# Moving attention bursts of the first tile pair to earlier places between its matmul groups

## The chip, the cores and the metric

The kernel runs on one core of one Trainium2 chip. The metric is the device time of one execution in microseconds (us). Changed and unchanged kernel are compared by the medians of their runs.

## The reference

Chunked attention feeds a feed-forward layer. Eight batches, 8 heads, 576 positions, head size 64; every chunk of 64 positions attends only to itself.

```python
scores = scale * np.matmul(q_c, k_c.transpose(0, 1, 2, 4, 3))
scores = scores - np.max(scores, axis=-1, keepdims=True)
attn = np.exp(scores)
attn = attn / (np.sum(attn, axis=-1, keepdims=True) + 1e-09)
out = np.matmul(attn, v_c)
...
h = x @ w_in
g = np.where(pos, h, np.where(neg, 0.0, (h + beta) ** 2 / (4.0 * beta)))
return (g @ w_out).astype(np.float32)
```

`x` is the attention output as 4608 tokens by 512; `w_in` is 512 x 2048, `w_out` 2048 x 512; `pos` is h >= 1 and `neg` is h <= -1.

## The kernel before, in words

The tokens are cut into nine tiles of 512 (`t` = 0 to 8). Attention is done in 36 units: one unit is one tile and one pair of heads. Unit n has two parts on TensorE (PE in the profile): its scores (L480, 32 small matmuls) and, after a softmax on VectorE (DVE) and ScalarE (ACT), its values (L502, 32 small matmuls). Operands of the feed-forward layer are split into a high and a low part, so that each product of 128x128 by 128x512 takes three matmuls.

Tiles 0 to 2 are computed plainly (L625, L661). Tiles 3 to 8 are computed as three pairs, (3, 4), (5, 6), (7, 8), by a scheme with seven products of half size in place of eight. A pair has two stages:

- **h**, 56 groups (L918): for each of eight blocks p of `w_in`, seven groups of six matmuls. DVE and ACT turn the results into activations (L939, L945, L948, L949).
- **outputs**, 56 groups (L1124): for each of the seven products in `OUT_ORDER = ("P1", "P2", "P6", "P5", "P7", "P3", "P4")`, eight groups of six matmuls. ACT and DVE make the operands (L743, L747). After P7, the pieces of the next pair's operands are split between the groups as well.

So a pair has 112 groups, and the kernel calls the position just before group n its place n: places 0 to 55 lie in h, 56 to 63 in P1, 64 to 71 in P2, 72 to 79 in P6, 80 to 87 in P5, and so on. The weights of each group come from DRAM into a ring of ten buffers (`RING`). The Pool queue issues one load of 256 KB per group (L896 in h, L891 in the outputs) as soon as the group ten before it has ended.

The attention of later tiles is put between these groups in bursts. `turns` lists sixteen of them, from unit 20 on, and `between(t, n)` takes the next from the list when n is one of the places in `BURSTS`, first entry for the first pair, second for the second. A burst for units (n, n+2) consists of:

- PE: the values of unit n and the scores of unit n+2, 64 small matmuls in one go.
- DVE and ACT: the softmax of unit n+2: maximum (L536), its scaling (L541), eight exponentials with sums (ACT, L547), sum and reciprocal (L565, L566), multiplication (L571), transposition (L588). ACT copies the values of unit n out of PSUM (L743). DVE transposes q and k of unit n+3 (L456).
- DMA on SP's queue: v of unit n+2 (two, L398), q and k of unit n+4 (four each, L382), and four of the eight moves of the softmax result into the place where the values product reads it (`aT`, L580). The other four moves are on Pool's queue, among the ring loads.

The values of unit n+2 need the `aT` moves of both queues, two bursts later. q, k, v, aT, maxima and sums have two buffers each, the transposed q and k one, and the two PSUM banks `ps_a` are shared by scores and values.

Each engine works its instructions in a fixed order. It is found before the launch by a list scheduler (`Plan.emit`), which gives each step a cost and takes, on each engine, the step that stands first in program order among those that are ready in its own account of time. A step written for a later place can so be taken earlier on its engine, if everything ahead of it is not ready in that account.

Of the kernel before, what the change touches and what calls it, by code (L numbers as in the profile page):

```python
# [134 lines left out]
def kernel(  # L135
# [826 lines left out]
        return f"h_{f}", lambda: held["h"][:, f, :]  # L962

    LATER = -60
    BURSTS = ((10, 17, 24, 38, 45, 52, 59, 68), range(3, 53, 7))
    sums = {
        (name, p): dram.tile([P, 2, QC], F32R, name=f"sums_{name}_{p}")
        for name in OUT_ORDER for p in range(NQ)
# [320 lines left out]
    def burst(n, m):  # L1289
        some = [values_of(*AT[n])] if n is not None else []  # L1290
        if m is not None:
            some.append(scores_of(*AT[m]))
        attn_products(*some, lag=0.8)
        if m is not None:
            attn_softmax(*AT[m])
        if n is not None:
            attn_split(*AT[n])
        if m is not None and m > 3 * NP and m + 1 < ALL:
            attn_turn(*AT[m + 1])
        if n is not None and n + 2 < ALL:  # L1300
            load_heads(*AT[n + 2], "v")
        if m is not None and m + 2 < ALL:
            load_heads(*AT[m + 2], "qk")
# [46 lines left out]
    def between(t, n):  # L1350
        if turns and n in BURSTS[(t - ALONE - 1) // 2]:
            burst(*turns.pop(0))
# [80 lines left out]
```

## Time and profile before

| | us |
|---|---|
| median of 3 runs | 806.91 |
| lowest, highest | 805.44, 808.49 |
| the profiled execution's own time | 805.89 |
| its span, first to last instruction | 804.1 |

The span is that of the profiled execution, 1.8 us less than its own time. Starts in the rows are us from the start of the span. A PE row of a timeline merges matmuls that follow each other; its length reaches to the modelled end of the last one, so the pace is read from one start to the next.

### The profile page before, as it was taken

Reading aid. Unit: us, or ns where it says so; the run is one execution under the profiler, and the core shown is the slowest. Engines: PE = TensorE matmul, PEld = TensorE weight load, DVE = VectorE, ACT = ScalarE, POOL = GpSimd, SP = SyncE. Lnnn points to the kernel's source line nnn. Section 1 sums busy time; section 2 is a strip of 40 time slices with the busy share of each in tenths; the row PEclk is TensorE's granted clock in tenths of the full one; section 3 lists DMA queues with packets and bytes.
Section 4 is the critical chain, followed back from the end, with each engine's and each line's share of the span. In section 5 each row is a group of like instructions: output and inputs, shape, how many; then the busy total and the mean of one; then the engine's idle time right before and its main releaser. Section 6 shows DMA issues by size and latency. Waiting matters only on the chain.

```text
span 804.1 us, 16928 instructions
## 1 busy us (share of the span) xinstructions
PE 795.0 (99%) x5652; PEld 652.8 (81%) x5652; DVE 650.2 (81%) x1131; ACT 537.7 (67%) x1293; POOL 345.5 (43%) x606
## 2 busy tenths in 40 slices
PE   8999999999999999999999999999999999999997
PEld 8887788888888888888888788888888888888886
DVE  5999996768799996686899996777996955589962
ACT  5799975455576775687894665887845556686450
POOL 2122223565655464554455334545343334433340
PEclk9999999999999999999999999999999999999999
DMA  9899843887998897999999899977686896666775
GB/s 223 249 302 239 221 78 127 252 261 228 293 255 225 199 283 207 302 264 250 259 246 273 217 245 256 257 230 214 184 214 197 223 243 195 194 191 195 218 200 118
DMA packets 289495, 181.51 MB, mean 226 GB/s; under 512 B 242945, under 2 KB 254721, under 8 KB 289409
## 3 DMA queue, kind: packets, MB, share of 16 engines
q0 software_dynamic: 40640, 122.72, 48.0%
q1 hardware_dynamic: 244544, 56.93, 33.7%
q10 hardware_dynamic: 4224, 0.79, 0.6%
q8 instruction: 45, 0.74, 0.4%
q14 instruction: 42, 0.34, 0.1%
HBM read 133.17 MB, written 38.80 MB: 214 GB/s over the span
## 4 chain that ended last, share of the span: by engine, by line
PE 84%; DMA 5%; DVE 4%; SPq 3%; ACT 2%; issue 2%; POOL 1%; DVEq 0%; POOLq 0%; ACTq 0%
PE ps_o L1124 17%; PE ps_o L661 15%; PE ps_h L625 15%; PE ps_h L918 13%; PE ps_o L918 13%; PE ps_h L1124 7%; PE ps_a L502 2%; SPq L382 2%; DVE new_wi L747 2%; PE ps_a L480 2%; DMA v_sb<-in_v_dram 1%; DMA k_sb<-in_k_dram 1%; DMA words<-in_moe_w_in_dram 1%; DMA q_sb<-in_q_dram 1%; DMA ring_r<-sums_P 1%
## 5 line engine op out<-in xcount | busy, mean ns | idle before, releaser
L747 DVE TENSOR_TENSOR new_wi<-new_wi,new_wi 128x512 fp32r<-128x512 f32 (+2 forms) x191 | 121.4, 668 | 13.7 <-ACT new_wi L743 12.0
L743 ACT CAST new_wi<-new_wi 128x512 fp32r<-128x512 f32 x157 | 94.3, 626 | 56.8 <-DVE new_wi L747 28.9
L625 PE MATMUL ps_h<-xh,parts 128*128 128x512 f32 x384 | 129.8, 398 | 0.0
L661 PE MATMUL ps_o<-parts,gh 128*128 128x512 f32 x384 | 118.2, 389 | 0.0
L580 POOL DMA_DIRECT2D aT<-e x96 | 50.6, 534 | 80.4 <-DVE r L636 46.0
L625 PEld LDWEIGHTS ps_h<-xh,parts 128*128 128x128 f32 x384 | 72.0, 188 | 16.0
L661 PEld LDWEIGHTS ps_o<-parts,gh 128*128 128x128 f32 x384 | 72.1, 188 | 15.0
L661 PE MATMUL ps_o<-parts,gl 128*128 128x512 f32 x192 | 74.7, 389 | 0.0
L949 DVE SCALAR_TENSOR_TENSOR new_wi<-h,new_wi 128x512 f32<-128x512 f32 x63 | 42.3, 683 | 26.1 <-ACT new_wi L948 26.1
L547 ACT ACTIVATE e<-ps_a,mx 128x64 f32<-128x64 f32 x168 | 50.8, 327 | 11.3 <-DVE mx L541 8.2
L948 ACT ACTIVATE new_wi<-new_wi 128x512 f32<-128x512 f32 x84 | 51.2, 627 | 1.2
L625 PE MATMUL ps_h<-x_parts,parts 128*128 128x512 f32 x128 | 50.1, 391 | 0.9 <-DVE x_parts L610 0.9
L945 ACT ACTIVATE new_wi<-h 128x512 f32<-128x512 f32 x63 | 39.4, 632 | 17.0 <-DVE h L939 17.0
L644 ACT CAST gh<-r 128x512 fp32r<-128x512 f32 x48 | 29.8, 620 | 30.0 <-DVE r L636 18.9
L661 PEld LDWEIGHTS ps_o<-parts,gl 128*128 128x128 f32 x192 | 36.0, 188 | 7.5
L747 DVE TENSOR_TENSOR new_wi<-new_wi 128x512 f32<-128x512 f32 (+2 forms) x64 | 39.4, 629 | 0.5
L636 DVE SCALAR_TENSOR_TENSOR r<-ps_h,r 128x512 f32<-128x512 f32 x48 | 32.6, 680 | 8.8 <-ACT r L635 8.6
L646 DVE TENSOR_TENSOR gl<-r,gh 128x512 fp32r<-128x512 f32 x48 | 32.7, 683 | 8.0 <-ACT gh L644 5.8
L1124 PE MATMUL ps_o<-new_wi,new_wo 128*128 128x512 f32 x156 | 37.6, 390 | 0.0
L580 POOL DMA_DIRECT2D aT<-x x48 | 24.7, 519 | 29.6 <-issue 13.8
L632 ACT ACTIVATE r<-ps_h 128x512 f32<-128x512 f32 x48 | 29.0, 604 | 11.8 <-PE ps_h L625 11.8
L547 ACT ACTIVATION_READ_ACCUMULATOR e<-ps_a,mx 128x1 f32 x168 | 36.7, 218 | 0.0
(232 smaller groups left out, 2074.9 us busy)
## 6 DMA issues: line engine op xcount, KB each, us to landing
ring_r<-combos POOLq DMA_DIRECT2D x36, 256.0 KB, 3.6
new_wo<-sums_P POOLq DMA_DIRECT2D x36, 256.0 KB, 3.2
new_wi<-combos POOLq DMA_DIRECT2D x34, 256.0 KB, 4.2
new_wi<-sums_P POOLq DMA_DIRECT2D x34, 256.0 KB, 3.5
ring_gh<-combos POOLq DMA_DIRECT2D x33, 256.0 KB, 3.7
ring_gl<-combos POOLq DMA_DIRECT2D x33, 256.0 KB, 3.8
ring_gh<-sums_P POOLq DMA_DIRECT2D x33, 256.0 KB, 3.9
ring_gl<-sums_P POOLq DMA_DIRECT2D x33, 256.0 KB, 3.4
```

The source lines that it names most:

```text
L547: nc.scalar.activation(out=e3[:, n, :], in_=sc[:, n // 4, n % 4, :], func=AF.Exp, bias=mx[:, n, :], scale=SCALE, accum_out=sm[:, n, :],)
L580: queues[queue].dma_start(out=aT[b:b + Q, to], in_=x[a:a + Q, of])
L625: nc.tensor.matmul(out=ps, lhsT=weight["wi", j][:, half, kc * P:(kc + 1) * P], rhs=x, start=(kc == 0 and i == 0), stop=(kc == KC - 1 and i ...
L646: plan.add("dve", 0.6, lambda: nc.vector.tensor_tensor(out=gl, in0=now(r), in1=gh.bitcast(F32), op=ALU.subtract), (rkey, ghkey), (glkey,), ...
L661: nc.tensor.matmul(out=acc, lhsT=x[:, cols], rhs=weight["wo", j][:, half, :], start=(j == 0 and i == 0), stop=(j == NF - 1 and i == 2),)
L743: "act", cost, lambda: nc.scalar.copy(out=out(), in_=src()), reads, writes, ahead=ahead
L747: plan.add("dve", cost, lambda: nc.vector.tensor_tensor(out=out(), in0=one(), in1=two(), op=op), reads, writes, port=True, ahead=ahead)
L918: nc.tensor.matmul(out=ps, lhsT=w()[:, at:at + P], rhs=y(), start=name in FRESH and i == 0 and k == 0, stop=i == 1 and k == 2, skip_group_ ...
L945: plan.add("act", 0.52, lambda: nc.scalar.activation(out=now(r), in_=h(), func=AF.Relu, bias=0.5, scale=0.5), (hkey,), (rkey,), ahead=50)
L948: plan.add("act", 0.52, lambda: nc.scalar.square(out=now(r), in_=now(r)), (), (rkey,), ahead=50)
L949: plan.add("dve", 0.6, lambda: nc.vector.scalar_tensor_tensor(out=now(r), in0=h(), scalar=1.0, in1=now(r), op0=ALU.max, op1=ALU.min), (hke ...
L1124: nc.tensor.matmul(out=acc, lhsT=w[:, half, b], rhs=x(), start=name in alone and p == 0 and k == 0, stop=p == NQ - 1 and k == 2, skip_grou ...
```

## The change

One tuple: the places of the eight bursts in the first pair, tiles 3 and 4.

```diff
     LATER = -60
-    BURSTS = ((10, 17, 24, 38, 45, 52, 59, 68), range(3, 53, 7))
+    BURSTS = ((10, 17, 24, 31, 38, 45, 52, 59), range(3, 53, 7))
```

The bursts are handed out in order, so the fourth, for units (23, 25), goes from place 38 to 31, the fifth from 45 to 38, the sixth from 52 to 45, the seventh, (26, 28), from 59 (in P1) to 52 (in h), and the eighth, (27, 29), from 68 (in P2) to 59 (in P1). The second pair's places stay.

## Rows read from the trace of the kernel before

**Rows 1.** The page: busy time and share by engine, and PE's granted clock.

```profile
PE 795.0 (99%) x5652; PEld 652.8 (81%) x5652; DVE 650.2 (81%) x1131; ACT 537.7 (67%) x1293; POOL 345.5 (43%) x606
PEclk9999999999999999999999999999999999999999
```

**Rows 2.** PE's waits over the whole span: us in total, times, longest (last of six, the only one after 100 us).

```profile
PE ps_o L1124 <- DVE new_wi L747: 0.2, 1, 0.2
```

**Rows 3.** PE's timeline, first pair: start, us, what, [idle before].

```profile
315.68 0.84 PE L918 MATMUL ps_h<-lows,new_wo 128*128 128x512 f32 x3
...
317.04 0.61 PE L661 MATMUL ps_o<-parts,gh 128*128 128x512 f32 x2
...
322.48 0.84 PE L918 MATMUL ps_h<-lows,new_wo 128*128 128x512 f32 x3
...
345.65 0.69 PE L502 MATMUL ps_a<-aT,v_sb 64*64 64x64 f32 x32
...
356.49 0.69 PE L502 MATMUL ps_a<-aT,v_sb 64*64 64x64 f32 x32
...
374.03 1.64 PE L918 MATMUL ps_h<-new_wi,ring_gh 128*128 128x512 f32 x6
375.51 1.52 PE L918 MATMUL ps_h<-new_wi,ring_r 128*128 128x512 f32 x6
376.96 0.69 PE L502 MATMUL ps_a<-aT,v_sb 64*64 64x64 f32 x32
...
437.97 0.69 PE L502 MATMUL ps_a<-aT,v_sb 64*64 64x64 f32 x32
...
441.92 2.98 PE L1124 MATMUL ps_o<-new_wi,new_wo 128*128 128x512 f32 x12
444.74 0.61 PE L1124 MATMUL ps_o<-new_wi,new_wi 128*128 128x512 f32 x2
445.52 2.56 PE L1124 MATMUL ps_o<-new_wi,new_wi 128*128 128x512 f32 x10 [0.17 <-DVE new_wi L747]
447.92 2.88 PE L1124 MATMUL ps_o<-new_wi,ring_r 128*128 128x512 f32 x12
450.63 1.52 PE L1124 MATMUL ps_o<-new_wi,ring_gh 128*128 128x512 f32 x6
...
486.00 0.84 PE L918 MATMUL ps_h<-low,new_wi 128*128 128x512 f32 x3
```

**Rows 4.** Busy us by stretch: PE, PEld, DVE, ACT, POOL, clock, DMA share, GB/s.

```profile
356.40:367.30 10.90, 10.90 (x108) 9.08 (x108) 8.63 (x16) 9.23 (x29) 5.82 (x12) 1.00 1.06 260
367.30:376.90 9.60, 9.60 (x43) 7.56 (x41) 5.34 (x8) 6.29 (x12) 5.34 (x11) 1.00 1.08 274
376.90:387.80 10.90, 10.90 (x107) 8.83 (x107) 8.63 (x16) 9.27 (x29) 4.20 (x8) 1.00 0.85 219
...
423.00:437.90 14.90, 14.90 (x125) 12.21 (x124) 14.82 (x28) 7.49 (x25) 8.38 (x16) 1.00 1.10 264
```

**Rows 5.** SP queue's timeline from the second burst of the pair on.

```profile
348.58 1.25 SPq L398 DMA_DIRECT2D v_sb<-in_v_dram  x2
...
356.98 3.61 SPq L580 DMA_DIRECT2D aT<-x  x4
360.69 1.08 SPq L398 DMA_DIRECT2D v_sb<-in_v_dram  x2
...
368.59 3.01 SPq L580 DMA_DIRECT2D aT<-e  x4
377.68 0.95 SPq L398 DMA_DIRECT2D v_sb<-in_v_dram  x2
```

**Rows 6.** DMA issues between 367 and 378 us: count, KB, median us to landing.

```profile
ring_gh<-combos POOLq DMA_DIRECT2D x2, 256.0 KB, 5.3
...
aT<-e SPq DMA_DIRECT2D x4, 32.0 KB, 5.2
```

**Rows 7.** DVE's timeline in the third burst of the pair, its idle time.

```profile
362.94 0.17 DVE L565 TENSOR_SCALAR sm<-sm 128x8 f32<-128x8 f32 x1 [1.83 <-ACT e L547]
```

## The prediction

> **What bounds the kernel now.** I read the page first. PE is busy for 795.0 of 804.1 us and its granted clock stays at full, the 2.4 GHz level, in all forty slices [rows 1]; so the question is only whether PE has idle time that a move can give back or cause. PE's list of waits has six entries, and only one is later than 100 us: 0.2 us on DVE in an output group [rows 2]. The reader is to see that nothing in the pairs waits on the attention.
>
> A busy PE can still hide idle time shorter than a matmul, because its ends are modelled. So I went to PE's timeline and counted starts [rows 3]. The 24 matmuls of tile 2 from 317.04 to 322.48 take 5.44 us, 0.2267 each, so a group of six takes 1.36 us. Two bursts seven groups apart start at 345.65 and 356.49, 10.84 us; less 7 x 1.36 = 9.52 a burst costs PE 1.32 us. The first pair reaches from 315.68 to 486.00, 170.32 us. In it lie 112 groups (152.32), those 24 matmuls (5.44), and nine bursts (11.88): eight of its own and, at 437.97, the one for units (28, 30), which is written for place 3 of the second pair and was taken far sooner. Sum 169.64. All idle time of PE in the stage is therefore 0.68 us, and I find most of it [rows 3]: two matmuls from 444.74 to 445.52 take 0.78 instead of 0.45 (0.33, the wait on DVE), the twelve from 441.92 take 2.82 instead of 2.72 (0.10), the six from 374.03 take 1.48 instead of 1.36 (0.12).
>
> **What the change moves.** Bursts are alike and are handed out in order. For PE, the eight places before and after differ in one: 31 in place of 68. The order of units does not change. So the change adds one burst before group 31, takes one away before group 68, and between the two everything on PE is 1.32 us later; after group 68 it is where it was. PE's work: +1.32 - 1.32 = 0.
>
> *DVE and ACT.* The same seven groups cost DVE 8.63 us with a burst and 5.34 without, ACT 9.23 and 6.29 [rows 4]: a burst is 3.3 us of DVE and 2.9 of ACT. The stretch from place 31 to 38, now 9.6 us with 5.34 of DVE, becomes 10.9 with 8.6, like its neighbours, which have no PE wait and where DVE even stands idle 1.83 us for the exponentials [rows 7]. The cover is this slack of 2.3 us; were it gone, the 3.3 us of DVE would push back activations, which the output operands need only after place 56. In the outputs, DVE is full around the removed burst, 14.82 of 14.9 us [rows 4], and it is DVE that PE waits for at 445.52. With 3.3 us less to do before, DVE is there earlier, and the 0.33 and 0.10 go: -0.4 us. Bounds: 0 (scheduler refills the hole) and -0.68 (all idle time of the stage). I take -0.4.
>
> *SP's queue.* Each burst puts 14 DMAs on it, and it works them in order. The `aT` moves, which the values product two bursts later waits for, stand behind v, q and k there. This is the one resource that has less room after the change. Place 31 falls at 356.49 + 10.84 = 367.33. Its `aT` moves are issued from 356.98 to 360.59 [rows 5]; a move lands 5.2 us after its issue [rows 6], the last of the four is issued about 0.9 before the end, so it lands near 364.9, 2.4 us early. Place 38 falls at 378.17; its moves end at 371.60, landing near 371.60 - 0.75 + 5.2 = 376.05, 2.1 us early (before, they were needed one burst after 376.96, at 387.8 [rows 3]). From here on SP no longer has the pause between 371.60 and 377.68 [rows 5], and each round of 14 must fit in 10.84 us. A round took 12.11 us from 348.58 to 360.69 and 10.91 from 360.69 to 371.60 [rows 5]. With the short round the moves for places 45, 52 and 59 land near 387.0, 397.9 and 408.8, for products at 389.01, 399.85 and 410.69: always 1.9 us or more early. With the long one they land at 388.2, 400.3 and 412.4: 0.9 early, 0.4 late, 1.7 late. A late move stops the burst on PE and with it every group behind it, and nothing gives that back. Bounds: 0 and +1.7 us. I take 0: the long round fell where the DMA engines were full (a share of 1.06 and more), and already in the round from 376.9 the share was 0.85 [rows 4], though that one had its loads close behind each other too.
>
> *Pool's queue and the ring.* The burst's four `aT` moves on Pool stand among the ring loads. A ring load is issued when the group ten before has ended, and lands 5.3 us later in the full stretch [rows 6]; it has nine groups, 12.2 us, so 6.9 us are left. The moved burst can eat some of that, not all: 0.
>
> The Trainium skill, DMA: Bandwidth & Descriptors, section Issuing engines are not separate DMA queues, says that DMAs started by SP, ACT and Pool all run on the same 16 engines and interleave; by it, loads of a burst brought into h slow the ring loads there. By that rule alone PE would lose time only where a ring load needs over 12.2 us, and the sum would stay.
>
> **Sum.** 0 (PE) - 0.4 (DVE's stall) + 0 (SP) + 0 (ring) = -0.4 us. The profiled execution took 805.89 us, its span 804.1; it becomes 805.5. The median of the three runs is 1.0 above that execution, so I forecast 806.9 - 0.4 = 806.5. About 0.5%, 4.0 us, is what a measurement of this kernel can tell from no change, so this is "same".
>
> **Rivals.**
>
> *The hole is refilled.* The scheduler already took burst (28, 30) far ahead of its place. With place 68 empty it may take that burst, or (29, 31) too, into the outputs earlier, so that DVE there is as full as before and the stall stays. For it: the row at 437.97. Against it: nothing firm. 806.9 us. Chance 0.13.
>
> *SP falls behind (the other side).* The place is the burst at 52 or 59, which waits for the `aT` moves. With rounds of 12.1 us it costs up to 1.7 us: 808.6, still within 0.5%. It makes the kernel slower by 4.0 us from the point where 376.05 + 3 x round passes 410.69 + 4.0, a round of 12.9 us, over 0.9 us for each DMA issue; by 5 us it is 811.9. For it: two rounds in a row without a pause, one of them over 10.84. Against it: the four bursts at places 38 to 59 of before stood as close and ran without a PE wait on `aT` [rows 2]. Chance 0.08 for a loss below 4 us, 0.06 for more.
>
> *More idle time than the rows show.* The Trainium skill, Perfetto Trace Analysis, section Tensor Engine Instruction (MATMUL, LD_WEIGHTS), says that the end of a matmul in a profile is an estimate; by it the 99% proves nothing, and a gain of several us could hide in it. The pace of the starts leaves 0.68 us in the stage, whatever the ends are, and it is 1.36 per group where DVE is full as in the rest. A gain of 4 us would have to come from another stage: 802.5 us. Chance 0.02.
>
> **How the numbers follow.** The forecast has 0.71, the rivals 0.13, 0.14 and 0.02. Faster by over 0.5%: 0.02. Slower by over 0.5%: 0.06. The rest is same: 0.92. For the range, the runs of before reach from 1.5 below their median to 1.6 above it; a median lies further inside, so I take 1.6 for the spread on both sides. Below, the bound of -0.68 adds 0.3: 806.5 - 0.3 - 1.6 = 804.6. Above, the bounds of DVE's stall (0.4) and of SP (1.7) add 2.1: 806.5 + 2.1 + 1.6 = 810.2.
>
> **What would show it.** Right: L502 rows on PE near 367.3 and 378.2, none near 423; the same 170 us between the first L918 group of the first and of the second pair; DVE in the stretch after 367 at about 8.6 of 10.9 us; no wait of 0.3 us near 445. SP's pause before 377.68 is gone. Wrong: a PE wait ahead of L502 on `aT` (SP too slow), or on a ring buffer; the stall at 445 still there, with a burst close before it (refilled); a PE wait on DVE at the end of h, where bursts 45 to 59 meet the first output operands.

## The result, and the profile after

The changed kernel is slower: its median is 810.9 us over 13 runs (810.01 to 817.26) against 806.91 over 13 runs of the kernel before, 4.0 us less. By the medians that is a ratio of 1.0049; the ratio on record, worked out over all runs, is 1.0066 with a 95% interval of 1.0052 to 1.0079. The forecast was 806.5 with a range up to 810.2, and "slower by over 0.5%" had a chance of 0.06. The profiled execution, at 810.18 us one of the shorter ones, has a span of 808.4 us, 4.3 more than before. Six of the thirteen runs took 812.64 us or more; what they lost beyond this is not shown by any profile.

The page answers to [rows 1]: PE does the same work at the same clock, so the 4.3 us are time in which it had none.

```profile
PE 794.7 (98%) x5652; PEld 653.1 (81%) x5652; DVE 651.0 (81%) x1131; ACT 538.5 (67%) x1293; POOL 345.8 (43%) x606
...
PEclk9999999999999999999999999999999999999999
```

PE's list of waits (us in total, times, longest) answers to [rows 2]. The late wait on DVE is gone. In its place stand three waits ahead of L502, the values product.

```profile
PE ps_a L502 <- DMA q_sb<-in_q_dram: 2.8, 1, 2.8
...
PE ps_a L502 <- DMA aT<-x: 1.0, 1, 1.0
PE ps_a L502 <- DMA aT<-e: 0.7, 1, 0.7
```

PE's timeline shows where they fall; it answers to [rows 3].

```profile
315.25 0.84 PE L918 MATMUL ps_h<-lows,new_wo 128*128 128x512 f32 x3
...
366.90 0.69 PE L502 MATMUL ps_a<-aT,v_sb 64*64 64x64 f32 x32
...
367.99 0.73 PE L918 MATMUL ps_h<-new_wi,new_wo 128*128 128x512 f32 x2
...
376.29 1.52 PE L918 MATMUL ps_h<-new_wi,ring_r 128*128 128x512 f32 x6
378.48 0.86 PE L502 MATMUL ps_a<-aT,v_sb 64*64 64x64 f32 x29 [0.67 <-DMA aT<-e]
...
399.00 1.52 PE L918 MATMUL ps_o<-new_wi,new_wo 128*128 128x512 f32 x6
401.53 0.86 PE L502 MATMUL ps_a<-aT,v_sb 64*64 64x64 f32 x29 [1.01 <-DMA aT<-x]
...
411.17 1.52 PE L1124 MATMUL ps_o<-new_wi,ring_gh 128*128 128x512 f32 x6
415.47 0.86 PE L502 MATMUL ps_a<-aT,v_sb 64*64 64x64 f32 x29 [2.78 <-DMA q_sb<-in_q_dram]
...
416.78 0.50 PE L1124 MATMUL ps_o<-new_wi,ring_gl 128*128 128x512 f32 x1
...
448.22 2.88 PE L1124 MATMUL ps_o<-new_wi,new_wi 128*128 128x512 f32 x12
450.94 2.88 PE L1124 MATMUL ps_o<-new_wi,ring_r 128*128 128x512 f32 x12
...
489.02 0.84 PE L918 MATMUL ps_h<-low,new_wi 128*128 128x512 f32 x3
...
493.19 0.69 PE L502 MATMUL ps_a<-aT,v_sb 64*64 64x64 f32 x32
```

The moved burst, at 366.90, starts on time. Six matmuls start in 1.36 us, and the last one ahead of a burst takes 0.09 more, so the burst after 376.29 was due at 377.74 and began at 378.48: 0.74 late. In the same way the one after 399.00 lost 1.08 and the one after 411.17 lost 2.85: 4.67 us. The undisturbed burst takes 1.09 us from its first small matmul to the next group (366.90 to 367.99), the one at 415.47 takes 1.31: a burst that waited also runs some 0.2 longer. Why it does is not shown.

The balance of the stage, by the terms of the prediction: it now reaches from 315.25 to 489.02, 173.77 us, with 112 groups (152.32), the 24 matmuls of tile 2 (5.44) and eight bursts (10.56), since the burst for (28, 30) now runs at its own place, at 493.19. That leaves 5.45 us idle, against 0.68 before: 4.77 more. The stage began 0.43 earlier, and what follows it takes 319.38 us in place of 318.10, 1.28 more, which is nearly the 1.32 of the burst that left the stage. So 4.77 - 1.32 + 1.28 - 0.43 = 4.30, the whole difference of the spans.

SP's timeline answers to [rows 5]. One round is v, q, k and then the moves of `aT`.

```profile
335.10 1.12 SPq L398 DMA_DIRECT2D v_sb<-in_v_dram  x2
338.63 2.34 SPq L382 DMA_DIRECT2D q_sb<-in_q_dram  x4
...
349.19 1.08 SPq L398 DMA_DIRECT2D v_sb<-in_v_dram  x2
...
362.57 1.12 SPq L398 DMA_DIRECT2D v_sb<-in_v_dram  x2
...
372.43 2.56 SPq L580 DMA_DIRECT2D aT<-e  x4
375.09 1.08 SPq L398 DMA_DIRECT2D v_sb<-in_v_dram  x2
...
386.30 1.10 SPq L398 DMA_DIRECT2D v_sb<-in_v_dram  x2
...
397.09 0.94 SPq L398 DMA_DIRECT2D v_sb<-in_v_dram  x2
398.40 3.96 SPq L382 DMA_DIRECT2D q_sb<-in_q_dram  x4
402.45 5.02 SPq L382 DMA_DIRECT2D k_sb<-in_k_dram  x4
407.57 1.02 SPq L398 DMA_DIRECT2D v_sb<-in_v_dram  x2
408.69 3.23 SPq L580 DMA_DIRECT2D aT<-e  x4
```

From v to v the rounds take 14.09, 13.38, 12.52, 11.21 and 10.79 us; bursts are due every 10.84. The first round holds a pause of 2.4 us ahead of its q, at 338.63; from there to the end of these rows the queue never pauses for more than 0.9 us. The four moves issued from 372.43 landed by 378.38, a tenth of a microsecond before the burst at 378.48. In the last stretch the moves for the burst at 415.47 stand behind two loads of v and eight of q and k, and are issued from 408.69 to 411.92; the last landed at 415.23. The list of waits names q_sb there, but it is this landing that the start follows. Nor is it the softmax that is late: for the three bursts that waited, DVE had written the transposed exponentials at 365.56, 388.20 and 402.66, and SP issued their moves from 372.43, 394.17 and 408.69, 6.0 to 6.9 us later.

The stretch after the moved burst, and DMA issues between 367 and 378 us, answer to [rows 4, 6] (columns as there):

```profile
366.90:377.70 10.80, 10.80 (x107) 8.83 (x106) 8.64 (x16) 9.13 (x29) 5.74 (x12) 1.00 1.13 260
```

```profile
ring_gh<-combos POOLq DMA_DIRECT2D x2, 256.0 KB, 6.2
```

From 366.90 on DVE has 8.64 us of work in 10.80, as forecast. The DMA engines are full, with a share of 1.13 against 1.08 in the stretch after place 31 of before. These ring loads land 6.2 us after their issue, 5.3 in the same window before [rows 6], and PE does not wait on the ring.

### The profile page after: what moved, and what is told of

Same layout as the page of the kernel before. It is cut to its first block, busy times and chain, and to the rows that moved or that the text cites. A ratio compares the mean times of both kernels' runs of the same rounds, so it can differ in the third digit from the quotient of the medians.

```text
span 808.4 us, 16938 instructions
## 1 busy us (share of the span) xinstructions
PE 794.7 (98%) x5652; PEld 653.1 (81%) x5652; DVE 651.0 (81%) x1131; ACT 538.5 (67%) x1293; POOL 345.8 (43%) x606
## 4 chain that ended last, share of the span: by engine, by line
PE 85%; DMA 5%; ACT 5%; SPq 2%; DVE 1%; issue 1%; POOL 0%; ACTq 0%; DVEq 0%; POOLq 0%
PE ps_o L1124 20%; PE ps_o L661 14%; PE ps_h L625 14%; PE ps_o L918 12%; PE ps_h L918 12%; PE ps_h L1124 8%; PE ps_a L502 2%; DMA q_sb<-in_q_dram 2%; PE ps_a L480 2%; DMA aT<-x 1%; ACT e L547 1%; SPq L382 1%; DMA k_sb<-in_k_dram 1%; ACT words L334 1%; DMA words<-in_moe_w_in_dram 1%
## 5 line engine op out<-in xcount | busy, mean ns | idle before, releaser
L632 ACT ACTIVATE r<-ps_h 128x512 f32<-128x512 f32 x48 | 29.0, 605 | 12.9 <-PE ps_h L625 12.9
L580 POOL DMA_DIRECT2D aT<-x x48 | 24.7, 520 | 26.9 <-issue 13.2
```

Source lines behind the costliest of these rows:

```text
L580: queues[queue].dma_start(out=aT[b:b + Q, to], in_=x[a:a + Q, of])
```

## The experiments

Each is an edit of the changed kernel, compared with the kernel before on the same chip, whose median there was 807.04 us for four of them and 806.49 for the other four. The theory is that SP's in-order queue hands out the `aT` moves too late.

**Is it the density of the bursts?** The first kernel sets them eight groups apart, the last at 66.

```diff
-    BURSTS = ((10, 17, 24, 31, 38, 45, 52, 59), range(3, 53, 7))
+    BURSTS = ((10, 18, 26, 34, 42, 50, 58, 66), range(3, 53, 7))
```

> The changed kernel with the eight bursts evenly eight groups apart, at 10, 18, 26, 34, 42, 50, 58 and 66: the same number of bursts, 12.2 us apart in place of 10.84. Theory A: a round of 14 DMAs of 10.5 to 12.5 us fits, waits of 0 to 0.5 us in all, 806.3 to 807.3. Theory B: six bursts still stand in h and one early in the outputs, DVE and ACT are as full there, 808.5 or more. Theory C: the DMA engines get 12% more time per burst, so it predicts as A does.

Measured 806.68 us (12 runs), ratio 0.9995 (0.9982 to 1.0009), and no wait of PE on the attention in the pairs above 0.15 us. Eight groups apart would be 8 x 1.36 + 1.32 = 12.20 us, but by their starts on PE the bursts stand 12.20, 10.84, 10.84, 15.11, 11.03, 13.76 and 12.20 apart, since the scheduler took some of them a group or two sooner. So there is a gap again, behind the fourth:

```profile
369.09 0.69 PE L502 MATMUL ps_a<-aT,v_sb 64*64 64x64 f32 x32
...
384.20 0.69 PE L502 MATMUL ps_a<-aT,v_sb 64*64 64x64 f32 x32
```

SP's rounds take 12.91, 11.96, 10.98 and 10.19 us from v at 349.92. The earlier places are harmless when the queue gets 1.4 us more a round on average (12.28) and one gap; this run does not part the two.

The second experiment puts only the last burst back to 68.

```diff
+    BURSTS = ((10, 17, 24, 31, 38, 45, 52, 68), range(3, 53, 7))
```

> The changed kernel with the eighth burst back at its place of before, 68, and the fourth to seventh one place sooner. Theory A: the seven close rounds stay, so the waits of the fifth and seventh burst stay (0.74 and 1.08), and the last, 2.85 us, goes since SP has nine groups more: 808.0 to 808.8 us. Theory B: the wait belongs to the end of h, which is as crowded; 810 or more.

Measured 808.71 (12 runs), ratio 1.0023 (1.0007 to 1.0039). Its profile is of one of its longer runs (810.62). By the starts in it the first pair loses 0.16 at 379, 0.74 at 390 and 1.25 at 402, and the large last wait is gone. The arrears were there before place 59 and only grew to it.

The third keeps the burst at 31 and leaves the double gap behind it, between 31 and 45.

```diff
+    BURSTS = ((10, 17, 24, 31, 45, 52, 59, 66), range(3, 53, 7))
```

> The changed kernel with the pause put back, but one burst later than in the kernel before: places 10, 17, 24, 31, 45, 52, 59 and 66. If SP's queue only needs one double gap to work off its arrears (four close bursts, then four): at most 0.3 us of waits, 806.3 to 807.2. If it is the burst at place 31 by itself that is bad: 809 or more.

Measured 806.34 (10 runs), ratio 1.0003 (0.9992 to 1.0013). PE waits on no attention in the pairs; the stall on DVE near 445 is back with 0.22 us, and so is the early burst for (28, 30), at 438.47. SP's timeline of this kernel:

```profile
349.60 1.47 SPq L398 DMA_DIRECT2D v_sb<-in_v_dram  x2
...
362.82 1.09 SPq L398 DMA_DIRECT2D v_sb<-in_v_dram  x2
...
374.50 1.10 SPq L398 DMA_DIRECT2D v_sb<-in_v_dram  x2
...
383.23 2.42 SPq L580 DMA_DIRECT2D aT<-e  x4
388.99 0.94 SPq L398 DMA_DIRECT2D v_sb<-in_v_dram  x2
```

Two rounds in a row are too long again (13.22 and 11.68), but after the moves at 383.23 to 385.65 the queue stands still until 388.99: the gap has paid the arrears. Place 31 is not the harm; that no gap comes after it is. The second pair of the changed kernel fits this: its bursts also stand seven groups apart and its rounds are too long (12.22, 12.11 and 11.54 us from v at 496.65), but after these three there are no more q and k to load, and PE does not wait.

**Is it SP's queue?** All eight `aT` moves of the later tiles go to Pool's queue.

```diff
-                queue = "pool" if t == 1 or j else "sp"
+                queue = "pool" if t == 1 or t > ALONE or j else "sp"
```

> The changed kernel, with the four aT moves of each later burst issued on Pool's queue in place of SP's, beside the four that are there already; same bytes, same places. Theory A (SP's queue: the moves stand behind v, q and k, and a round of 14 DMAs takes longer than the 10.84 us between bursts): the moves leave soon after the softmax, PE's three waits ahead of L502 (0.74, 1.08, 2.85 us) go, 806.3 to 807 us. Theory B (the softmax itself is late, since DVE and ACT are full at the end of h): the waits stay, 810 to 811. Theory C (all 16 DMA engines are full, so that the moves land late from whichever queue): at least 2 us of waits stay, 808.5 or more, or ring loads come late in their place.

Measured 814.19 (6 runs), ratio 1.008 (1.0057 to 1.0102): the gain that the theory of SP expected did not come, and ring loads came late, as the third theory allowed. SP itself kept pace at once, with v at 347.91, 358.75, 369.59 and 380.44, 10.84 or 10.85 apart, and of the waits ahead of L502 in the first pair one of 1.30 us at 414 is left. But Pool's timeline shows the moves waiting for landings of ring loads, and ring loads behind them:

```profile
387.99 0.50 POOL L580 DMA_DIRECT2D aT<-e  x1 [1.77 <-DMA ring_gh<-combos]
388.54 0.56 POOL L896 DMA_DIRECT2D ring_r<-combos  x1
```

The waits are of the program's making, as the last section tells. PE then waits for the ring, 1.07 us at 392, and in the second pair:

```profile
PE ps_h L918 <- DMA ring_gl<-combos: 1.8, 1, 1.8
```

That SP keeps pace with ten DMAs a round agrees with the theory that its own load makes it late; and the run shows that Pool's queue, as this program works it, is no place for more.

**What makes a round so long?** First the bytes: q and k of units 25 to 30 bring only half of their chunks, so the other half of those units' scores is not computed from this input.

```diff
-                eng.dma_start(
-                    out=dst[r:r + Q],
-                    in_=rows.rearrange("c (e p) d -> p c e d", p=Q),
-                )
+                cs = CT // 2 if 25 <= turn(t, g) <= 30 else CT
+                eng.dma_start(out=dst[r:r + Q, :cs], in_=rows.rearrange("c (e p) d -> p c e d", p=Q)[:, :cs])
```

> The changed kernel; the q and k loads of units 25 to 30 bring only the first half of the chunks (the other half keeps old data), so SP issues as many DMAs, with half the packets and bytes in those eight. Theory count (what makes a round on SP long is the number of issues): rounds as before, 4.7 us of waits ahead of L502, about 810.9 us. Theory bytes (an issue is held up until the shared DMA engines have worked off what stands before it): rounds of 9 us or less, waits of 0 to 0.7, 806.3 to 807.3 us.

Measured 806.15 (10 runs), ratio 0.9992 (0.9982 to 1.0001), no wait in the first pair. SP's v are issued at 348.67, 359.11, 369.96 and 380.79, with pauses between. The same 14 DMAs fit when eight of them carry half. The DMA share from 366.90 to 377.70 is 0.88.

Then the traffic of others: ring loads bring half their columns for 42 groups of the first pair's h, the other half of those weights staying what the buffer held, and nothing on SP is touched. (The expectation speaks of each pair; the edit acts in the first alone, where the bursts in question lie.)

```diff
+        some = T // 2 if 14 <= step < 56 else T
...
-            out=ap().bitcast(F32), in_=combos[d][:, n, :].bitcast(F32)
+            out=ap()[:, :some].bitcast(F32), in_=combos[d][:, n, :some].bitcast(F32)
```

> The changed kernel with half the columns of each ring load left out for groups 14 to 55 of each pair's h stage (the other half keeps old data). SP's own DMAs stay as they are. Theory bytes, with all queues sharing the DMA engines: SP's rounds shrink to 10 us or less, the waits ahead of L502 go except for 0 to 1 us, 806.3 to 807.5. Theory that only SP's own DMAs matter (count or bytes on its queue): rounds and waits as in the changed kernel, 810 to 811.5.

Measured 806.03 (10 runs), ratio 0.9992 (0.9983 to 1.0002), no wait in the first pair. SP's timeline, and a window of it (columns as in [rows 4]):

```profile
368.97 2.00 SPq L398 DMA_DIRECT2D v_sb<-in_v_dram  x2
371.79 2.42 SPq L382 DMA_DIRECT2D q_sb<-in_q_dram  x4
374.30 2.04 SPq L382 DMA_DIRECT2D k_sb<-in_k_dram  x4
377.29 2.42 SPq L580 DMA_DIRECT2D aT<-e  x4
379.81 2.13 SPq L398 DMA_DIRECT2D v_sb<-in_v_dram  x2
```

```profile
366.90:377.70 10.80, 10.80 (x107) 8.79 (x107) 8.59 (x17) 9.13 (x29) 5.75 (x12) 1.00 0.79 177
```

Four loads of k take 2.04 us to issue; in the changed kernel's rounds they took 3.04 to 5.02. SP's own DMAs are untouched, so its issues take longer because of what else the DMA engines carry: at a share of 0.79 the first four rows sum to 8.9 us, and the queue waits for its next turn; in the changed kernel a round without a pause takes 10.8 to 13.4. In what way full engines hold up an issue on SP, no run here shows.

Then the count: each load of q and k of units 25 to 30 is cut in two of half the size, the same bytes in 22 DMAs a round.

```diff
+                some = ((0, CT // 2), (CT // 2, CT)) if 25 <= turn(t, g) <= 30 else ((0, CT),)
+                for a, z in some:
+                    eng.dma_start(out=dst[r:r + Q, a:z], in_=rows.rearrange("c (e p) d -> p c e d", p=Q)[:, a:z])
```

> The changed kernel with each of the q and k loads of units 25 to 30 cut into two DMAs of half the chunks: the same bytes and packets, 22 DMAs in a round in place of 14. Theory count: eight more issues at 0.4 us or more each, rounds 3 us longer, at least 6 us more of waits ahead of L502, 815 us or more. Theory bytes: rounds as in the changed kernel, waits of 4 to 6.5 us, 810 to 813 us.

Measured 821.05 (4 runs), ratio 1.0173 (1.0156 to 1.0191). SP's timeline:

```profile
392.67 1.08 SPq L397 DMA_DIRECT2D v_sb<-in_v_dram  x2
393.84 5.14 SPq L384 DMA_DIRECT2D q_sb<-in_q_dram  x8
399.08 5.59 SPq L384 DMA_DIRECT2D k_sb<-in_k_dram  x8
...
407.28 1.08 SPq L397 DMA_DIRECT2D v_sb<-in_v_dram  x2
```

In this round a half load takes 0.64 to 0.70 us, waits between issues included, and 22 issues take 14.6 us, against 8.9 for 14 in the kernel with half the ring loads. So the count has a price of its own: about 0.5 us for a load where the engines are not full (four of k in 2.04), up to 1.25 where they are (four in 5.02). By the first of these alone, an estimate from these rows, 22 issues take more than 10.84 us and 14 do not. Part of the 14.6 us is the program's own rule for its queues, told in the last section. The five waits ahead of the values in the first pair sum to 8.8 us, and after the two long ones PE also ran slow, which is told there too.

**The count by itself** was to be had from four transfers of 4 bytes each ahead of q of units 24 to 30.

```diff
+                nc.sync.dma_start(out=spare[i * Q:i * Q + 1, k:k + 1], in_=q[0, 0, i:i + 1, k:k + 1])
```

> The changed kernel with four DMAs of 4 bytes each put ahead of the q loads of units 24 to 30 on SP's queue; they load into a scratch tile that nothing reads. Orders of all other work are as in the changed kernel. Theory A with the count of issues as what makes a round long (0.6 to 0.9 us for each): rounds 2.4 to 3.6 us longer, waits at each of five bursts, 815 to 822 us. Theory A with the bytes and packets of q, k and v as what makes it long: under 1 us for a round, 811 to 814.

Measured 817.06 (4 runs), ratio 1.0127 (1.0102 to 1.0152). That lies where the theory of the count wanted it, but not for its reason: the waits in the first pair are 3.58 us, less than in the changed kernel, while the scores that the kernel before starts at 70.55 us start at 75.38, 4.8 later, where nothing was meant to change and PE's clock is 0.93 from 24 to 50 us against 1.00. The four small ones took 1.37 to 1.83 us to issue, but the loads of q behind them got shorter, 1.9 to 3.1. It is inconclusive, and why the kernel's beginning differs stays open.

## Why the prediction was wrong

- *PE's work: 0.* Right. The busy time is 794.7 and 795.0, and the moved burst stands at 366.90 (forecast 367.3).
- *DVE and ACT.* Right for h: 8.64 of 10.80 us, no wait on DVE. The stall of 445 is gone, as forecast: the twelve matmuls at 448.22, the ones that it struck before, take 2.72 us from start to start. Its 0.33 and 0.10 us are what the term of -0.4 stood for. But the cause is not shown to be the burst that left place 68. Two bursts left these outputs, that one and the one for (28, 30); with the last burst back at 68 and (28, 30) still late, no such stall stands in the profile either, and it is back in the kernel with the double gap, where (28, 30) is early. It does not always follow that burst: at eight groups apart (28, 30) is early too, without a stall.
- *"The hole is refilled."* It was not. The scheduler took the burst for (28, 30) in the second pair, the other way round.
- *The ring.* Right that PE does not wait on it. By the rule of the Trainium skill that was named there (DMA: Bandwidth & Descriptors, Issuing engines are not separate DMA queues), loads brought into h slow the ring loads; some do land later here, at 6.2 us against 5.3, still inside the 12.2.
- *SP's queue: the step that failed.* It took 0 and a bound of +1.7; it cost 4.67 us of waits and with the bursts that ran longer 5.4. The mechanism was named as a rival and its size was wrong; of its places, 52 and 59 were right, but the burst at 38, which was to have 2.1 us to spare, was late as well.

  The bound was worked out from two pieces of the trace before. One was the time of the moves for place 38: forecast to land near 376.05, they landed at 378.38, 2.3 us later, though the stage began 0.43 sooner. In the trace before, the two rounds from v at 348.58 ended 23.02 us later [rows 5] and a pause came behind them; here the same two rounds from 349.19 took 25.90 (13.38 and 12.52) up to the next v, without a pause. The first of them is 13.2 to 13.4 us long in this trace and in those with the last burst at 68 and with the double gap, against 12.11. The edit does not explain this: up to 366 us, ahead of the burst that moved, PE, DVE, ACT, Pool and SP work the same instructions in the same order in these three traces as in that of before. SP is some 2.3 us behind the kernel before by then already (v at 362.57 against 360.69, less the 0.43). Each kernel has one profile, so whether this is the spread between executions stays open; what the edit took away is the pause that made up for it.

  The other piece was the three rounds after it: from 378.38 to 415.23 they took 12.28 each, against the 12.11 of the long case. So 412.4 became 415.2, and of the 2.8 us the first landing carries 2.3. Without these 2.3 the same three rounds would have cost a little over 2 us, an estimate: more than the bound of 1.7, less than half of what came. The 12.9 us a round named as the point for a loss of 4 held for moves that start at 376.05; starting 2.3 later, 12.3 was enough.
- *Why 0 was taken.* The rival's "two rounds in a row without a pause, one of them over 10.84" misread its own figures: 12.11 and 10.91 are both over it. The long round was put down to a place where the DMA engines were full, and the share of 0.85 after it [rows 4] was read as relief, in a round that "had its loads close behind each other too". It had not. In the trace before, v of 377.68 [rows 5] was issued by 378.63, and SP then stood still for 2.39 us:

```profile
381.02 1.92 SPq L382 DMA_DIRECT2D q_sb<-in_q_dram  x4
```

With no gap the share stays over 1 (1.13 from 366.90, 1.01 from 377.70, 1.12 from 389.50 to 400.40), and half the ring traffic, or half of the bytes of q and k, takes the whole loss away. "The four bursts at places 38 to 59 of before stood as close" was a poor witness too: they came after the gap, with no arrears, and SP paused in their rounds as well, 2.39 us here and 1.51 ahead of q at 391.86. The double gap at 31 to 45 shows that a gap is enough for this; why the rounds behind one are shorter is not shown.

The Trainium skill, DMA: Bandwidth & Descriptors, section Issuing engines are not separate DMA queues, says that starting DMAs on several engines saves only the sequencer's time to start them, and calls that usually small beside the DMA. That they share the engines agrees: less ring traffic from Pool shortened SP's issues. Beside the DMA one start is the smaller part here too, some 0.5 to 1.25 us against medians of 4.3 to 6.4 us to landing. But one queue works its starts one after the other: 14 of them take 8.9 to 13.4 us of a 10.84 us period, and this is what set the end.

What stays open is how much of the loss a different order on SP would save, with the `aT` moves ahead of v, q and k, since these were ready 6.0 to 6.9 us before they were issued. It was not tried. No version beat the kernel before by a measurable amount; PE has only 0.68 us of idle time in this stage there.

## What to carry to other kernels

When periodic work is set closer together, add up its in-order DMA queue over a whole run of periods at the new density, and take the time of an issue from stretches where the DMA engines are as full as they will be; a round that had a pause near it is too cheap a model. A gap in a hand-written order may be what lets a queue catch up, so look for what is idle in it before it is closed. Arrears in such a queue grow silently: they began here before the edit's place, reached TensorE one burst after it and cost most four bursts after it.

## What the hardware showed that was not expected

With the split loads PE stood idle for 3.02 us ahead of 382.31 and 4.10 ahead of 410.43, and afterwards the groups started at little more than half pace. PE's timeline and two windows of that kernel:

```profile
382.31 0.95 PE L501 MATMUL ps_a<-aT,v_sb 64*64 64x64 f32 x29 [3.02 <-DMA aT<-e]
...
383.71 2.61 PE L917 MATMUL ps_o<-new_wi,ring_gh 128*128 128x512 f32 x6
...
388.15 1.07 PE L917 MATMUL ps_o<-new_wi,new_wo 128*128 128x512 f32 x4
```

```profile
383.50:387.50 4.00, 4.00 (x28) 3.11 (x20) 2.58 (x5) 1.88 (x9) 0.54 (x1) 0.58 0.52 94
...
411.80:414.50 2.70, 2.70 (x15) 2.10 (x9) 1.77 (x3) 1.73 (x3) 0.00 (x0) 0.50 0.46 78
```

The granted clock was 0.58 and 0.50 in these stretches, that is, mostly or wholly the level of 1.2 GHz, and 1.00 from 373 to 377 and from 388 to 392 us. Twelve matmuls from 383.71 to 388.15 took 4.44 us in place of 2.72, 1.72 lost on top of the wait. The Trainium skill, TensorE: Matmul & The Clock Gate, Part 1: The HAM clock gate, says that the clock follows how busy PE has been and falls to half when it has not; the trace agrees. The waits of up to 2.85 us in the changed kernel were not followed by such a stretch; its clock stays at 1.00 in every window after them.

In the kernel with all moves on Pool, the move at 387.99 waited 1.77 us for the ring load issued at 380.60, which landed at 387.70. By the semaphores in the trace this is a rule of the program, not a trait of Pool: the transfers of each queue signal eight semaphores in turn, and one is issued only when the transfer eight before it on the queue has landed. SP's queue has the same rule. In the changed kernel the load of q at 352.19 stood 0.83 us for the move issued at 344.31, which landed at 352.18. There such waits come to only 1.8 us from 338 to 412 us, and nearly all the rest of the long rounds is the issues themselves; with the split loads they come to 5.1 us in the four rounds from 351.41.
